# Attention with chunk selection and a top-1 expert layer: longer runs for the loads of Q, K and the second expert weights, a regrouping on GpSimd, and two weight tensors

## The chip, the cores and the metric

The kernel runs on one core of one Trainium2 chip. The metric is the device time of one execution in microseconds. Before the change nine runs were timed; their median is the time before.

A core has five engines that run side by side: TensorE (PE; its weight loads are PEld), VectorE (DVE), ScalarE (ACT), GpSimd (POOL) and SyncE (SP), which here only issues transfers. The transfers of all queues go over 16 transfer engines (DMA).

## The reference

Inputs: q, k, v of 4 batches x 8 heads x 768 tokens x 64; a gate of 512 x 8; for each of 8 experts a first weight matrix of 512 x 1024 and a second one of 1024 x 512, all float32.

```
k_min, k_max = min and max of k over each chunk of 32 tokens
ub    = sum_d max(q * k_min, q * k_max)          # a bound for each query and chunk
top   = the 6 chunks with the largest bound, among chunks not after the query's own
attn  = softmax of q k^T / 8 over the tokens of those chunks up to the query
x     = attn @ v, heads side by side             # 3072 tokens x 512
e     = argmax(x @ w_gate);  g = softmax(x @ w_gate)[e]
out   = g * (relu(x @ w1[e]) @ w2[e])            # one expert per token
```

## The kernel before

Attention goes by pairs of heads: 16 pairs (4 batches x 4), one step of the loop at line 886 for each (pair 0 is written out above it). Within a step for pair i the program interleaves three pairs. For pair i it computes scores (TensorE, L427), their exponentials (ScalarE, L432), the causal mask of the diagonal blocks (GpSimd, L440) and the product with V (TensorE, L455). For pair i+1 it computes the bounds (TensorE, L374), the choice of chunks (VectorE) and the turn of V (L276). For pair i+2 it turns K and Q with TensorE transposes (L227, L245), takes the chunk minima and maxima out of PSUM with VectorE (L235, L236), and evicts K and Q with ScalarE and VectorE (L239, L250, L265). Scores come in seven tiles a pair, units 0 to 6; only tiles 0, 1, 5 and 6 have masks.

K, Q and V of a pair are loaded by SyncE (L201 to L218), one transfer per head. Partition p of tile t holds token 128 t + p, so every run in memory is one row of 64 floats, 256 B. K and Q have two buffers each, by the parity of the pair: pair i+4 is loaded as soon as pair i+2 has been turned, two steps before its use. Even pairs use a tile of their own; odd pairs use space in `w_all` that belongs to the last expert and is filled with weights later.

The expert weights are loaded by GpSimd, which converts them to bf16 on the way (L186 to L195): 32 loads, four per expert, each of 1 MB in HBM; the first two of an expert bring w1 in rows of 1024, the last two w2 in rows of 512. All land in the one tensor `w_all`. A list gives each load a slot; there are four slots a step:

```
many = [4 + n * 44 // 19 for n in range(19)]
wq = [0, 1, 2, 3] + many + [48, 50, 51, 52, 54, 55, 56, 57, 58]
```

When a batch's four pairs are done, its tokens are routed: logits, gate and rank (VectorE, with small matmuls), and then six scatters (GpSimd, L561) write the rows of x to `xs_dram`, sorted by expert. For the first three batches they are spread over the next batch's steps.

GpSimd and TensorE run in the order that the program is written in; so do VectorE and ScalarE in the first part, and VectorE in the loop. GpSimd's order in a step is: three masks (tiles 0 and 1 of pair i), two casts `q_c` (L257), a cast `q_d` (L268), then by slots a weight load and a scatter, the mask of tile 5, again weight load and scatter, the two masks of tile 6, and again.

The expert layer takes tiles of 128 sorted rows: GpSimd gathers them (L666), SyncE turns them with a transfer (L678), `up` multiplies by w1 (L699), ScalarE applies relu (L707), a transfer turns the result (L711), `down` multiplies by w2 two tiles later (L755), ScalarE scales by the gate (L761), and GpSimd scatters the rows to the output (L739). Which expert a tile belongs to is read from a table into a register, which selects the weights at run time. The last tile of the 28 that always run is handled in halves (L703 to L736).

Of the kernel before, what the change touches and what calls it, by code (L numbers as in the profile page):

```python
# [24 lines left out]
def kernel(  # L25
# [34 lines left out]
    VW = D + 1 + E  # L60
    LK = max(NT * 2 * D, 3 * XW // 2)
# [6 lines left out]
    w_all = wpool.tile([128, E * WE], BF16)  # L68
# [117 lines left out]
    def load_w(s_):  # L186
        e, n = divmod(s_, 4)
        if n < 2:
            dst = w_all[:, ds(e * WE + n * 2 * F, 2 * F)].rearrange("p (c f) -> p c f", c=2)
            src = moe_w1[e, ds(n * 256, 256)]  # L190
        else:
            dst = w_all[:, ds(e * WE + W1W + (n - 2) * 4 * DM, 4 * DM)].rearrange("p (c f) -> p c f", c=4)
            src = moe_w2[e, ds((n - 2) * 512, 512)]
        d = nc.gpsimd.dma_start(out=dst, in_=src.rearrange("(c p) f -> p c f", p=128))  # L194
        tc.keep_in_program_order(d)  # L195
# [5 lines left out]
    def load(i, nm):  # L201
        if i >= NP:
            return
        b, hp = divmod(i, HP)
        if nm in "kq" and i % 2:
            at = (E - 1) * WE + (W1W + 4 * DM if nm == "k" else 2 * F)
            t_ = w_all[:, ds(at, NT * 4 * D)].bitcast(FP32).rearrange("p (t a d) -> p t a d", a=2, d=D)
        elif nm == "k":
            t_ = ld.tile([128, LK], FP32, tag=nm, name=nm)
            t_ = t_[:, 0:NT * 2 * D].rearrange("p (t a d) -> p t a d", a=2, d=D)  # L210
        elif nm == "q":
            t_ = ld.tile([128, NT, 2, D], FP32, tag=nm, name=nm)
        else:
            t_ = V[i % 3][:, :, 1 + E:1 + E + 2 * D].rearrange("p t (a d) -> p t a d", d=D)
        for hd in range(2):
            nc.sync.dma_start(out=t_[:, :, 1 - hd if nm == "v" else hd, :],
                              in_=dict(k=k, q=q, v=v)[nm][b, 2 * hp + hd].rearrange("(t p) d -> p t d", p=128))
        st[i][nm] = t_  # L218

    def prep_steps(i):  # L220
# [3 lines left out]
        def k_t(hf):  # L224
            pt = ps_m.tile([128, 384], FP32, tag="m")
            for t in range(3):
                nc.tensor.transpose(pt[:, ts(t, 128)], s["k"][:, 3 * hf + t], ident_f[:])  # L227
            s[f"kp{hf}"] = pt

        def k_red(hf):  # L230
            if hf == 0:
                s["kmx"] = work.tile([128, NCH], FP32, tag="kmx", name="kmx")
                s["kmn"] = work.tile([128, NCH], FP32, tag="kmn", name="kmn")
            v_ = s[f"kp{hf}"][:].rearrange("p (c w) -> p c w", w=CH)
            nc.vector.tensor_reduce(s["kmx"][:, ts(hf, 12)], v_, AX.X, ALU.max)  # L235
            nc.vector.tensor_reduce(s["kmn"][:, ts(hf, 12)], v_, AX.X, ALU.min)  # L236

        def k_out(hf, hd):
            nc.scalar.activation(kte[0:64, hd, ts(hf, 384)], s[f"kp{hf}"][64 * hd:64 * hd + 64, :],  # L239
                                 AF.Copy, bias=0.0, scale=0.125)  # L240

# [6 lines left out]
        def q_v(hf):  # L248
            qT = s[f"qT{hf}"] = work.tile([128, 384], FP32, tag=f"qT{hf}", name="qT")
            nc.vector.tensor_copy(out=qT[:], in_=s[f"qp{hf}"][:])  # L250
# [12 lines left out]
        def q_va(hf):  # L263
            qT = s[f"qT{hf}"] = work.tile([128, 384], FP32, tag=f"qT{hf}", name="qT")
            nc.scalar.activation(qT[:], s[f"qp{hf}"][:], AF.Copy)  # L265
# [35 lines left out]
        def first(idle):  # L301
# [11 lines left out]
            for hf in range(2):  # L313
                s[f"qT{hf}"] = work.tile([128, 384], FP32, tag=f"qT{hf}", name="qT")
                qA = s[f"qA{hf}"] = work.tile([128, 384], FP32, tag=f"qA{hf}", name="qA")
                nc.scalar.activation(qA[:], s[f"qp{hf}"], AF.Relu)
                if hf == 0:
                    nc.scalar.activation(s["qT0"][:], s["qp0"], AF.Copy)
                else:
                    nc.vector.tensor_copy(out=s["qT1"][:], in_=s["qp1"])  # L320
# [139 lines left out]
    def norm(i, hf):  # L460
        b, hp = divmod(i, HP)
        s = st[i]
        if hf == 0:
            s["lgt"] = work.tile([128, 3, 2, 2, E], FP32, tag="lgt", name="lgt", bufs=2)
            if hp == 0:
                bst[b]["lg"] = work.tile([128, 3, 2, E], FP32, tag="lg", name="lg", bufs=2)
                for h in range(2):
                    if b % 2 == 0 or h:
                        t_ = work.tile([128, 3, XW], BF16, tag=f"xrow{b % 2}{h}", name="xrow")[:]
                    elif b < B - 1:  # L470
                        at = (E - 1) * WE + W1W
                        t_ = w_all[:, ds(at, 3 * XW)].rearrange("p (t x) -> p t x", x=XW)
# [109 lines left out]
    def table(first):  # L582
# [25 lines left out]
        nc.vector.tensor_scalar(woff[:, cols], ej[:], float(WE), None, ALU.mult)  # L608
# [43 lines left out]
    def gather(j):  # L652
# [9 lines left out]
        elif j == 2:  # L662
            spare = ld.tile([128, 2, 768], BF16, tag="q", name="spare")
# [27 lines left out]
    def up(j):  # L691
        _, (wo,) = nc.values_load_multi_w_load_instructions(
            woff[0:1, j:j + 1], engines=[PE], min_val=0, max_val=(E - 1) * WE,
# [3 lines left out]
        for c in range(NDC):  # L697
            for fh in range(F // 512):
                nc.tensor.matmul(ph[:, fh, :], lhsT=xT[:, c, :],  # L699
                                 rhs=w_all[:, ds(wo + (c * F + fh * 512), 512)],  # L700
                                 start=(c == 0), stop=(c == NDC - 1), skip_group_check=True)
        h_ = work.tile([128, F], BF16, tag="P", bufs=6)
        if j == JM - 1:  # L703
            nc.scalar.activation(h_[:, 0:512], ph[:, 0], AF.Relu)
            nc.vector.tensor_scalar(h_[:, 512:F], ph[:, 1], 0.0, None, ALU.max)
        else:
            nc.scalar.activation(h_[:].rearrange("p (a f) -> p a f", a=2), ph[:], AF.Relu)  # L707
# [16 lines left out]
    def down_last():  # L724
# [4 lines left out]
        for n in range(2):  # L729
            py = (ps_m.tile([128, w], FP32, tag="m", name="py") if n else  # L730
                  ps_o.tile([128, w], FP32, tag="o", name="py"))
            for c in range(NFC):
                nc.tensor.matmul(py[:], lhsT=hT[:, c, :], rhs=w_all[:, ds(wo + (W1W + c * DM + n * w), w)],
# [12 lines left out]
    def down(j, mid=None):  # L746
# [5 lines left out]
        for c in range(NFC):  # L752
            if mid and c == 5:
                mid()
            nc.tensor.matmul(py[:], lhsT=hT[:, c, :], rhs=w_all[:, ds(wo + (W1W + c * DM), DM)],  # L755
# [12 lines left out]
    many = [4 + n * 44 // 19 for n in range(19)]  # L768
    wq = [0, 1, 2, 3] + many + [48, 50, 51, 52, 54, 55, 56, 57, 58]

    def weights(slot):
        for n in range(NW):
            if wq[n] == slot:
                load_w(n)
# [18 lines left out]
    with tc.manual_schedule(engines=MAN):  # L793
# [5 lines left out]
        with tc.manual_schedule(engines={DVE, ACT}):  # L799
# [3 lines left out]
            load(1, "v")  # L803
            load(2, "k")
            load(2, "q")
# [11 lines left out]
            p["k_t"](1)  # L817
            load(3, "k")
# [9 lines left out]
            p["q_t"](1)  # L828
# [258 lines left out]
```

## Time and profile before

| what | value |
| --- | --- |
| median of 9 runs | 367.48 us (361.55 to 373.47) |
| the profiled execution | 367.15 us, span 365.4 us |
| mean granted clock of TensorE | 0.973 |
| busy in the span | TensorE 325.4, weight loads 243.2, ScalarE 199.5, GpSimd 177.0, VectorE 175.1 us |
| packets | 137148, 59.92 MB |
| attention, to about 250 us | 16 steps, 12.9 to 16.8 us each between 20 and 216 us |
| expert layer, from about 250 us | 28 tiles, 3.45 us each at 318 to 350 us |

How to read the lines: a slice row has 40 digits, each the busy share of 1/40 of the span in tenths. A window line has the stretch, its length, the busy time of each engine with its instructions, the granted clock, the share of the transfer engines' time in which packets were under way (outstanding packets can make it more than 1), and the GB/s. A waits line names the engine and line that waited, what it waited for, the total, the count and the longest. A timeline line has start, duration, engine, line, operation, output and inputs, and in brackets the idle time before it and what ended it. "issue" stands for a wait that the profile shows no cause for.

### The profile page before, as it was taken

What the parts mean: (1) busy time and instruction counts of PE and PEld (TensorE: products, weight loads), DVE (VectorE), ACT (ScalarE), POOL (GpSimd) and SP (SyncE); (2) the same over time, 40 slices, a digit from 0 to 9 for tenths busy, and PEclk for the clock granted to TensorE, in tenths of its full rate; (3) what the DMA queues carried; (4) which work ended last, traced back from release to release, by engine and by line L of the source; (5) the groups of instructions that cost most, each with busy time, mean ns of one, the idle gap of its engine ahead of it and who ended that gap; (6) DMA issues with size and microseconds to landing.
All of it is one profiled execution on the core that took longest, in us unless ns stands there. A gap on an engine that the chain in (4) does not pass through costs nothing.

```text
span 365.4 us, 13315 instructions
## 1 busy us (share of the span) xinstructions
PE 325.4 (89%) x5321; PEld 243.2 (67%) x5333; DVE 175.1 (48%) x725; ACT 199.5 (55%) x339; POOL 177.0 (48%) x316
## 2 busy tenths in 40 slices
PE   7899897999999999999999869558999979999980
PEld 3689787898899889889989758435434434444440
DVE  6779476375875777876686737204700000000010
ACT  3778675565866865866774825212244434445440
POOL 7355326052376354366546386640656554654331
PEclk9999999899999999999999999968999999999996
DMA  9999999686989998999976795971989798989830
GB/s 178 194 207 165 218 197 201 128 153 127 173 160 158 196 186 158 169 163 162 200 142 109 148 125 111 183 165 31 180 178 226 165 179 215 186 225 170 207 98 25
DMA packets 137148, 59.92 MB, mean 164 GB/s; under 512 B 121723, under 2 KB 129917, under 8 KB 137088
## 3 DMA queue, kind: packets, MB, share of 16 engines
q0 software_dynamic: 17536, 29.42, 43.1%
q1 hardware_dynamic: 119552, 29.65, 42.5%
q8 instruction: 44, 0.72, 0.8%
q14 instruction: 16, 0.13, 0.1%
HBM read 56.14 MB, written 10.51 MB: 182 GB/s over the span
## 4 chain that ended last, share of the span: by engine, by line
PE 51%; issue 22%; POOL 11%; DVE 6%; DMA 4%; ACT 3%; POOLq 1%; SPq 0%; DVEq 0%; ACTq 0%
PE po L455 22%; PE ps L427 9%; PE ubp L374 5%; POOL out_dram L739 4%; PE vwp L292 3%; PE pt L276 3%; PE pt L245 3%; PE pt L227 3%; DMA xs_dram<-xrow,sli 2%; POOL xs_dram L561 2%; ACT KTE L239 2%; POOL xg L666 1%; ACT P L432 1%; DMA q<-in_q_dram 1%; POOL spare L666 1%
## 5 line engine op out<-in xcount | busy, mean ns | idle before, releaser
L432 ACT ACTIVATE P<-ps 128x768 f32<-128x768 f32 x144 | 89.6, 666 | 69.0 <-PE ps L427 53.2
L455 PE MATMUL po<-V,P 128*64 128x73 f32 x2688 | 108.8, 230 | 13.6 <-issue 7.5
L455 PEld LDWEIGHTS po<-V,P 128*64 128x64 f32 x2688 | 101.9, 138 | 22.5 <-issue 11.3
L440 POOL TENSOR_SCALAR_AFFINE_SELECT P<-P 128x256 f32<-128x256 f32 x90 | 34.6, 406 | 54.1 <-ACT P L432 40.3
L427 PE MATMUL ps<-QSB,KTE 128*64 128x384 bf16 (+2 forms) x576 | 55.9, 296 | 0.5 <-issue 0.5
L755 PE MATMUL py<-w_all,hT 128*128 x211 | 50.4, 379 | 0.9 <-DMA hT<-h__5481 0.3
L239 ACT ACTIVATE KTE<-pt 64x384 bf16<-64x384 f32 x64 | 30.9, 483 | 16.5 <-DVE kmn L236 9.2
L755 PEld LDWEIGHTS <-hT 128*128 128x128 bf16 x216 | 21.0, 98 | 26.9 <-issue 1.2
L561 POOL DMA_INDIRECT xs_dram<-xrow,sli x21 | 21.5, 1026 | 28.1 <-DVE cnt L586 14.0
L699 PE MATMUL ph<-w_all,KTE 128*128 x116 | 29.6, 394 | 3.3 <-issue 1.8
L427 PEld LDWEIGHTS <-KTE 128*64 128x64 bf16 x576 | 29.1, 111 | 4.8 <-issue 3.6
L402 DVE COPY QSB<-pm 24x768 bf16<-24x768 bf16 x30 | 16.5, 550 | 17.7 <-PE pm L398 17.2
L699 PE MATMUL ph<-w_all,QSB 128*128 x102 | 24.3, 379 | 0.6 <-issue 0.5
L194 POOL DMA_DIRECT2D w_all<-in_moe_w_dram x32 | 24.6, 770 | 0.2
L480 DVE RECIPROCAL rec<-po 128x6 f32<-128x6 f32 x32 | 6.2, 195 | 38.3 <-PE po L455 24.5
L374 PE MATMUL ubp<-KS,qT 128*64 128x48 f32 x384 | 24.1, 224 | 0.5 <-issue 0.4
L699 PEld LDWEIGHTS <-KTE 128*128 128x128 bf16 x120 | 11.9, 100 | 18.4 <-issue 4.8
L374 PE MATMUL ubp<-KD,qA 128*64 128x48 f32 x384 | 23.7, 222 | 0.4 <-issue 0.4
L739 POOL DMA_INDIRECT out_dram<-V,ti x14 | 13.8, 985 | 18.7 <-ACT V L761 17.4
L374 PEld LDWEIGHTS ubp<-KS,qT 128*64 128x64 f32 x384 | 20.0, 137 | 3.3 <-issue 2.5
L374 PEld LDWEIGHTS ubp<-KD,qA 128*64 128x64 f32 x384 | 20.1, 138 | 0.5 <-issue 0.5
L276 PE MATMUL pt<-ident_f,V 128*128 128x128 f32 x96 | 16.2, 283 | 3.1 <-ACT qT L265 2.6
(208 smaller groups left out, 474.2 us busy)
## 6 DMA issues: line engine op xcount, KB each, us to landing
w_all<-in_moe_w_dram POOLq DMA_DIRECT2D x32, 512.0 KB
V<-in_v_dram SPq DMA_DIRECT2D x32, 192.0 KB
k<-in_k_dram SPq DMA_DIRECT2D x16, 192.0 KB
q<-in_q_dram SPq DMA_DIRECT2D x16, 192.0 KB
w_all<-in_k_dram SPq DMA_DIRECT2D x16, 192.0 KB
w_all<-in_q_dram SPq DMA_DIRECT2D x16, 192.0 KB
xs_dram<-xrow,sli POOLq DMA_INDIRECT x21
out_dram<-V,ti POOLq DMA_INDIRECT x14
```

Source lines behind the costliest of these rows:

```text
L194: d = nc.gpsimd.dma_start(out=dst, in_=src.rearrange("(c p) f -> p c f", p=128))
L239: nc.scalar.activation(kte[0:64, hd, ts(hf, 384)], s[f"kp{hf}"][64 * hd:64 * hd + 64, :], AF.Copy, bias=0.0, scale=0.125)
L276: nc.tensor.transpose(pt[:, ts(t, 128)], V[i % 3][:, 3 * hf + t, 1 + E:1 + E + 2 * D], ident_f[:])
L374: nc.tensor.matmul(pu[c:c + CW, 3 * hf + t].rearrange("p a n -> p (a n)"), lhsT=s[f"{nm}{hf}"][:, ds(t * 128 + c, CW)], rhs=w_[:], start=( ...
L427: nc.tensor.matmul(pv[c:c + CW, hd, :], lhsT=kte[:, hd, ds(kb * 128 + c, CW)], rhs=qsb[:, hd, ds(qb * 384 + 384 - w, w)], start=True, stop ...
L432: nc.scalar.activation(P[:, :, ds(c0, w)], pv, AF.Exp)
L440: nc.gpsimd.affine_select(out=pd, in_=pd, pattern=[[0, 2], [1, 128]], compare_op=ALU.is_ge, fill=0.0, base=0, channel_multiplier=-1)
L455: nc.tensor.matmul(po[c:c + CW, t].rearrange("p a d -> p (a d)")[:, ds(hd * VW, VW)], lhsT=P[:, hd, ds(col + c, CW)], rhs=vt[:, kb, ds((1 ...
L561: d = nc.gpsimd.indirect_dma_start(out=xs_dram[:], out_offset=bass.IndirectOffsetOnAxis(ap=sli[:, u:u + 1], axis=0), in_=bst[b][f"xrow{u % ...
L699: nc.tensor.matmul(ph[:, fh, :], lhsT=xT[:, c, :], rhs=w_all[:, ds(wo + (c * F + fh * 512), 512)], start=(c == 0), stop=(c == NDC - 1), sk ...
L739: d = nc.gpsimd.indirect_dma_start(out=out[:], out_offset=bass.IndirectOffsetOnAxis(ap=ti[:], axis=0), in_=y, in_offset=None, bounds_check ...
L755: nc.tensor.matmul(py[:], lhsT=hT[:, c, :], rhs=w_all[:, ds(wo + (W1W + c * DM), DM)], start=(c == 0), stop=(c == NFC - 1))
```

## The change

- K and Q are loaded in longer runs. K of a head comes in two transfers: tokens 0 to 511 with four rows of 64 in a run, so that partition p holds tokens 4p to 4p+3, and tokens 512 to 767 with two. Q comes in two transfers with three rows each. In memory a run is 1024, 512 or 768 B.
- For pairs from 1 on the runs land in a buffer with heads outermost (`outer`), and GpSimd copies them into one with the heads side by side for each row (`inner`, by `spread`); pair 0 is written there directly, in pieces of 256 B. There is now one buffer to land in and one to turn from, for K and for Q. The copy for pair i+3 stands in step i, behind the transposes of pair i+2, and the load of pair i+4 follows it.
- Since tokens are now spread over partitions in runs, the transposed columns are out of order; the evictions of K and Q write them with steps, and the chunk reductions read them with steps. K's two PSUM tiles hold 512 and 256 columns instead of 384 each.
- `w_all` is split into `w1_all` and `w2_all`. w2 is loaded so that a partition gets four neighbouring rows, 8 KB in one run; relu therefore reads its PSUM tile with a step of four, to bring the hidden units into the same order.
- The weight loads go out in another order (first weights, then second; those of the last expert that lie over the K and Q buffers last), and in evenly spaced slots: 1, 2, 4, 6, 8, 10, 11, 13, ... 47, 49, 51, 53, 55, 57.
- In the last tile the two halves of the output swap the PSUM pools that they use.

The diff, cut to its core:

```diff
-    w_all = wpool.tile([128, E * WE], BF16)
+    w1_all = wpool.tile([128, E * W1W], BF16)
+    w2_all = wpool.tile([128, E * W1W], BF16)
...
-            dst = w_all[:, ds(e * WE + W1W + (n - 2) * 4 * DM, 4 * DM)].rearrange("p (c f) -> p c f", c=4)
-            src = moe_w2[e, ds((n - 2) * 512, 512)]
+            dst = w2_all[:, ds(e * W1W + (n - 2) * 4 * DM, 4 * DM)]
+            src = moe_w2[e, ds((n - 2) * 512, 512)].rearrange("(p c) f -> p (c f)", p=128)
...
+            for lo, n in RUNS[nm]:
+                tok_ = src[128 * lo:128 * (lo + n)]
+                if i == 0:
+                    nc.sync.dma_start(out=t_[:, lo:lo + n, hd], in_=tok_.rearrange("(p t) d -> p t d", t=n))
+                else:
+                    nc.sync.dma_start(out=t_[:, hd, lo:lo + n].rearrange("p t d -> p (t d)"),
+                                      in_=tok_.rearrange("(p t) d -> p (t d)", t=n))
+    RUNS = dict(k=((0, 4), (4, 2)), q=((0, 3), (3, 3)))
...
+    def spread(i, nm):
+        if i >= NP:
+            return
+        dense = st[i][nm]
+        st[i][nm] = inner(nm)
+        nc.gpsimd.tensor_copy(out=st[i][nm].rearrange("p t a d -> p a t d"), in_=dense)
...
+            v_ = s[f"kp{hf}"][:].rearrange("p (s c w) -> p c s w", s=n, w=CH // n)
+            nc.vector.tensor_reduce(s["kmx"][:, c], v_, AX.XY, ALU.max)
...
+            nc.scalar.activation(kte[0:64, hd, ds(128 * lo, 128 * n)].rearrange("p (w s) -> p s w", s=n),
+                                 s[f"kp{hf}"][64 * hd:64 * hd + 64, :].rearrange("p (s w) -> p s w", s=n),
...
+            nc.vector.tensor_copy(out=in_order(qT[:]), in_=as_read(s[f"qp{hf}"][:]))
...
-            nc.scalar.activation(h_[:].rearrange("p (a f) -> p a f", a=2), ph[:], AF.Relu)
+            nc.scalar.activation(h_[:].rearrange("p (a c f) -> p a c f", a=2, c=4),
+                                 ph[:].rearrange("p a (f c) -> p a c f", c=4), AF.Relu)
...
-            py = (ps_m.tile([128, w], FP32, tag="m", name="py") if n else
-                  ps_o.tile([128, w], FP32, tag="o", name="py"))
+            py = (ps_o.tile([128, w], FP32, tag="o", name="py") if n else
+                  ps_m.tile([128, w], FP32, tag="m", name="py"))
...
+    first_w = [4 * e + n for e in range(E) for n in (0, 1)]
+    second_w = [4 * e + n for e in range(E) for n in (2, 3)]
+    order_w = first_w[:-1] + second_w[:-2] + first_w[-1:] + second_w[-2:]
...
+            if 1 + n * 56 // (NW - 1) == slot:
+                load_w(order_w[n])
...
             if pj:
                 pj["k_t"](0)
                 pj["k_t"](1)
-                load(i + 4, "k")
...
             scores(i, 2)
+            spread(i + 3, "k")
+            load(i + 4, "k")
...
+            spread(i + 3, "q")
+            load(i + 4, "q")

             scores(i, 4)
```

## The prediction

> **What bounds the kernel now.** I read the page's busy shares and slices first, then the transfer queues, then windows cut at each attention step (from one head pair's bound matmuls, line 374, to the next's), then the waits and timeline of the stretches that stood out.
>
> ```profile
> PE 325.4 (89%) x5321; PEld 243.2 (67%) x5333; DVE 175.1 (48%) x725; ACT 199.5 (55%) x339; POOL 177.0 (48%) x316
> ...
> PE   7899897999999999999999869558999979999980
> ...
> PEclk9999999899999999999999999968999999999996
> DMA  9999999686989998999976795971989798989830
> ```
>
> TensorE is the bound; the transfer engines are close to full beside it, and no other engine is over 55%. So a cheaper transfer pays only where TensorE stands still because of transfers. The windows show where that may be (columns: stretch, length, busy time of PE, PEld, DVE, ACT, POOL, granted clock, transfer share, GB/s):
>
> ```profile
> 31.80:46.70 14.90, 13.29 (x303) 11.93 (x302) 8.99 (x36) 9.25 (x17) 7.11 (x18) 1.00 1.19 213
> ...
> 60.30:77.00 16.70, 14.37 (x303) 13.55 (x302) 8.98 (x36) 9.38 (x17) 5.52 (x14) 0.90 0.71 133
> 105.00:118.10 13.10, 13.03 (x302) 12.13 (x304) 9.05 (x36) 9.64 (x19) 8.78 (x19) 1.00 0.98 179
> ...
> 198.90:215.70 16.80, 12.70 (x294) 11.12 (x294) 10.93 (x47) 8.52 (x16) 9.80 (x15) 1.00 0.81 147
> 229.40:249.40 20.00, 12.62 (x130) 7.82 (x131) 3.15 (x11) 4.11 (x6) 8.94 (x11) 0.75 0.71 150
> ```
>
> A step with the same 303 matmuls takes 13.1 us when nothing disturbs it (105.0) and 14.9 or 16.7 us early on. The waits of TensorE from 44 to 77 us say what for:
>
> ```profile
> PE po L455 <- issue: 2.8, 2, 2.3
> PE vwp L292 <- issue: 1.4, 1, 1.4
> ```
>
> "issue" is a wait for nothing shown. Both long ones (1.42 us before 45.16, 2.33 us before 64.65) fall while the transfer share is over 1 and SyncE needs 9.66 us to issue one pair of V loads (29.64). I read them as TensorE's own instructions coming late through the full transfer engines. It is a reading; no row proves it.
>
> **Part 1, the transfers.** The queue rows:
>
> ```profile
> DMA packets 137148, 59.92 MB, mean 164 GB/s; under 512 B 121723, under 2 KB 129917, under 8 KB 137088
> ...
> q0 software_dynamic: 17536, 29.42, 43.1%
> q1 hardware_dynamic: 119552, 29.65, 42.5%
> ```
>
> From 105 to 118.1 us q1 moved 4704 packets in 42.1% of 13.1 us: 5.5 us of all 16 engines per step, 18.8 ns x engine per 256 B packet (13.6 B/ns). Weights from 20 to 45 us: 3.01 MB, 5.74 loads of 0.52 MB, in 72.6% of 25 us, so 3.16 us each; one reads 1 MB, 20.7 B/ns. K and Q of a step are 786 KB: 3.6 us at the first rate, 2.4 us at the second; packets of 512 to 1024 B lie between, I take 3.0. That is 0.6 us a step off the transfers. W2 in 8 KB runs falls from 512 to 128 packets a load, and gets 0 to 10% cheaper by the same two rates.
>
> Of more weight is when the weights go. Slots (four a step): before 0,1,2,3,4,6,8 ... 54,55,56,57,58; after 1,2,4,6,8 ... 51,53,55,57. Two of the first four loads leave step 0 (6.3 us of transfers off the backlog at 30 to 60 us), and the last full step issues one load, not three. The middle gets denser, some 2.2 loads a step where 1.7 were: 7.0 us, with K and Q 3.0, V 1.8 (1536 packets) and a scatter or two of 0.5 comes to 12.3 us a step of 13.1, or 13.2 with K and Q at 3.6. So a loss there is bounded by 0.1 us x 8 steps, about +1; I take 0.
>
> A, early stalls: three steps from 31.8 to 77 us last 45.2 us; at 13.2 each they would last 39.6. Between 0 and 5.6 us are to be had; I take -4.0, as the transfer share there (1.19, 1.13) should come to about 1.
> B, end of attention: three loads issued at 223.5 to 225.5 fill the engines until 233.8 (q0 89.5% from 229 to 238 us), and TensorE loses 0.46, 0.21 and about 1.1 us to "issue" there and some 1.3 us behind it. 0 to -3; taken -2.0. The next stretch, 238.7 to 244.7 us, has 24 matmuls with gaps near 0.7 us between them, beside gathers and transposes that the change leaves alone: taken 0, but up to -7 with the clock of 0.5 to 0.75 that follows.
> D, step 13: GpSimd issues a weight load at 209.73, then two scatters, and its masking at 213.14 is what TensorE waited 2.80 us for. That load moves one slot up, where GpSimd waits 4.34 us for the gate anyway. -0.8 (one issue, 0.77 us); bounds 0 and -1.1.
>
> **Part 2, the regrouping on GpSimd.** Thirty copies of 128x768 f32. Nearest rows: cast 64x384 0.496 us (L257), mask 128x256 0.406, memset 64x768 0.73. From the first two, 0.7 ns per element over 0.23 us: 0.77 us; with strides I take 0.9, bounds 0.7 and 2.0 (four L257 casts). 30 x 0.9 = 27 us on an engine that is busy 177 of 365. Its cover is the idle time between casts and masks (3.9 us at 119.3). Each copy waits for its loads, the transposes that read the old data, and GpSimd's order; masks, weight issues and scatters queue behind it, and the next K or Q load on SyncE waits for it. A load is now issued one step ahead instead of two, so 12 us cover its landing. Where scatters precede, the cover is thin:
>
> ```profile
> 118.38 0.94 POOL L257 CAST QSB<-qT 64x384 bf16<-64x384 f32 x2
> 123.23 0.50 POOL L268 CAST QSB<-qT 64x384 bf16<-64x384 f32 x1 [3.90 <-DMA xs_dram<-xrow,sli]
> 123.69 0.78 POOL L194 DMA_DIRECT2D w_all<-in_moe_w_dram  x1
> 124.78 1.05 POOL L561 DMA_INDIRECT xs_dram<-xrow,sli  x1 [0.30 <-issue]
> 127.06 1.25 POOL L440 TENSOR_SCALAR_AFFINE_SELECT P<-P 128x256 f32<-128x256 f32 x3 [1.24 <-ACT P L432]
> ```
>
> The cast waits for the scatters to land; after it now come weight issue, copy, scatter, copy: 123.73 + 0.78 + 0.9 + 1.35 + 0.9 = 127.7 where the mask is due at 127.06: 0.6 us late. The steps at 105, 159 and 171.9 have casts ending 2.1, 1.5 and 0.2 us earlier in their steps, so 0, 0 and 0.4. Steps 5 and 9 scatter without that wait, 0 to 0.3. G: +1.0 (bounds 0 and +9: with copies of 2.0 us the six steps lose 2.8, 0.7, 1.3, 2.6, 1.0, 1.0).
>
> **Part 3, the start.** K and Q of pair 0 need eight issues instead of four before TensorE can turn Q. An issue takes 0.52 us (1.04 for two): last one ends at 5.0 instead of 3.0. But 786 KB at the 215 GB/s of that stretch take until 5.7 anyway, and Q was awaited at 6.7: F +0.4, bounds 0 and +2.0. The copies of pair 1 end near 10.7 and 12.4 us by the same rate; its K transposes run at 12.21, its Q transposes at 16.81.
>
> **Part 4, reordered elements.** K evictions (L239, 0.483 us), Q evictions (L250, 0.557; L265, 0.487) and K reductions (0.552) keep their element counts but write or read with steps; relu (L707, 1.023 us) reads PSUM at every fourth element. The trace has no long stepped eviction; the nearest, the reciprocal of 128x6 at step 73, takes 0.195 us against 0.17 for six packed elements. So 0, and at the other end a doubling, which lies beside other work: ScalarE is busy 9.1 to 9.6 of 13.1 us a step, and a tile's transpose is issued at 322.83 for matmuls at 328.49, 5.7 us later with a transfer of 1.23 us to issue.
>
> [...]
>
> E, the tail: the last two output halves swap their PSUM pools.
>
> ```profile
> 353.31 0.69 ACT L761 ACTIVATE V<-py,xg 128x512 f32<-128x512 f32 x1 [0.23 <-PE ph L718]
> ...
> 354.05 2.31 PE L733 MATMUL py<-w_all,hT 128*128 x16 [0.99 <-ACT V L761]
> ```
>
> The first half now takes a free bank and starts at 353.1; the second, 1.15 us later, finds the old one evicted at 354.0: -0.95. A slower last relu (0.60 to 1.2 us) hides before the turn at 351.80. Splitting the weight tensors frees nothing: the last load has landed by 234, the first expert matmul runs at 245.9.
>
> **Sum.** A -4.0, B -2.0, D -0.8, E -0.95, F +0.4, G +1.0: -6.35. The profiled execution took 367.15 us (span 365.4), 0.33 below the median of 367.48, so 360.8 for it and 361 at the median. The nine runs spread from 361.55 to 373.47, so I call 1% what can be told from no change.
>
> A rule that speaks against A and B: the Trainium skill, "Runtime: NRT & Kernel Launch", Instruction fetch mechanics, says that fetches in 16 KiB blocks are hidden behind execution. The two gaps of 1.42 and 2.33 us under full transfers agree better with late fetches; by the rule A and B are nothing and the sum is 366.8.
>
> **Rivals.**
> 1. The stalls stay (A and B at 0): TensorE's gaps were not the transfers', or the denser middle brings as many as leave. For it: gaps at 207.4 and 208.1 us with the transfer share at 0.25. Time 367.15 - 0.35 = 366.8.
> 2. Slower: GpSimd becomes the pace in the six scatter steps. Place: the copy of Q ahead of the mask of the fifth score tile. Each microsecond past 127.06 in the example goes to TensorE, six times. It decides from 1.2 us more per step than planned (7.35 us: the gain of 6.35 and the 1 us already counted), by copies of 2 us or scatters landing later behind denser weights. At 2 us: 360.8 + 12 = 373. Against it: the L257 rate, and the other seven steps with copies have casts that end 1 us after they start and no scatter to wait for.
> 3. Faster still: the stretch 238.7 to 244.7 us also heals: 361 - 7 = 354.
>
> **Chances.** Forecast (356 to 363.8) 0.48; stalls stay (363.8 to 371) 0.24; GpSimd paces (over 371) 0.21; faster still 0.07. Faster by over 1% is below 363.8: 0.55; within 1%: 0.24; slower, above 371.2: 0.21. The range leaves out one in ten at each end: 354 (rival 3) to 374 (rival 2 at its price).
>
> **What will show it.** A: steps from 31.8 to 77 us near 13.3 us, "issue" waits of TensorE shorter. B: no matmul gaps from 228 to 235 us, q0 low there. G: copies of 0.7 to 1.0 us; TensorE's wait for masks (3.0 us before) up by about 1. E: no wait before the last 16 matmuls. Q1 with 32768 packets fewer. Wrong would make it: copies near 2 us, or copies waiting for loads longer than a step, or step times as uneven as before with less transfer share.

## The result and the profile after

The changed kernel takes 394.6 us (median of 10 runs, 391.1 to 400.57), beside 367.2 us for the kernel before (31 runs): a ratio of 1.079, interval 1.0748 to 1.0832. The forecast was 361.0 with a range of 354 to 374. The profiled execution took 389.96 us, span 388.2.

The runs below were made on four chips, and the median of the kernel before was 355 to 369 us by chip. So kernels are compared on one chip, by their ratio to the kernel before. Each ratio is taken from the fast runs of both kernels, and so differs a little from the ratio of the medians.

From the page after: the busy shares, the slices of TensorE, its clock and the transfers, and the queues.

```profile
PE 334.6 (86%) x5321; PEld 248.8 (64%) x5333; DVE 177.9 (46%) x725; ACT 229.8 (59%) x339; POOL 198.5 (51%) x346
...
PE   6887898898979889879898797795789999999994
...
PEclk9898999988989999999899899998699999999999
DMA  5755977958576889687668674547259999999971
...
DMA packets 101310, 59.94 MB, mean 154 GB/s; under 512 B 76667, under 2 KB 92029, under 8 KB 101248
...
q0 software_dynamic: 11392, 29.42, 38.8%
q1 hardware_dynamic: 89856, 29.66, 36.2%
```

The transfers became cheaper: 35838 packets fewer, both queues less busy. In q1 it is 29696 packets fewer, where 32768 were forecast; pair 0, which still lands in pieces of 256 B, is part of the difference. ScalarE gained 30.3 us of work (199.5 before), GpSimd 21.5 (177.0). TensorE's share fell, and the loss is in attention. The windows after, cut at the bounds of one pair and the next (stretch, length, PE, PEld, DVE, ACT, POOL, clock, transfer share, GB/s):

```profile
70.10:86.60 16.50, 14.65 (x302) 12.91 (x301) 9.10 (x36) 11.29 (x17) 7.18 (x16) 0.90 0.77 154
121.00:135.90 14.90, 13.06 (x303) 11.80 (x302) 9.02 (x36) 11.07 (x19) 9.53 (x17) 1.00 0.79 169
...
231.30:247.90 16.60, 12.35 (x297) 11.04 (x296) 11.32 (x47) 10.39 (x16) 9.13 (x14) 1.00 0.51 98
```

An undisturbed step (121.0) now takes 14.9 us for the same 303 matmuls, where it took 13.1, with the transfer engines at 0.79 instead of 0.98 and ScalarE at 11.1 us instead of 9.6. TensorE's waits from 11.7 to 248 us say for what:

```profile
PE pt L316 <- ACT qT L305: 20.3, 13, 1.6
PE pt L285 <- ACT KTE L272: 5.8, 12, 1.0
PE pt L316 <- ACT KTE L272: 2.3, 1, 2.3
PE po L495 <- issue: 1.6, 1, 1.6
```

Before, from 8.7 to 216 us, the waits for ScalarE's evictions of K and Q were 3.0 us together:

```profile
PE pt L276 <- ACT qT L265: 2.6, 4, 0.7
...
PE pt L276 <- ACT KTE L239: 0.4, 1, 0.4
```

Now they are 28.4. The groups of ScalarE, by form, before (L239 evicts K, L265 evicts Q) and after (L272, L305):

```profile
L239 ACT ACTIVATE KTE<-pt 64x384 bf16<-64x384 f32 x64 | 30.9, 483 | 16.5 <-DVE kmn L236 9.2 <-PE ubp L374 6.1 <-PE pt L227 0.7
...
L265 ACT ACTIVATE qT<-pt 128x384 f32<-128x384 f32 x15 | 7.3, 487 | 1.8 <-PE pt L245 1.5
```

```profile
L272 ACT ACTIVATE KTE<-pt 64x512 bf16<-64x512 f32 x32 | 42.4, 1324 | 18.9 <-DVE kmn L268 18.5
...
L272 ACT ACTIVATE KTE<-pt 64x256 bf16<-64x256 f32 x32 | 14.6, 457 | 0.5
...
L305 ACT ACTIVATE qT<-pt 128x384 f32<-128x384 f32 x15 | 10.3, 687 | 1.7 <-PE pt L285 1.7
```

The same 24576 columns of K cost 57.0 us instead of 30.9. The form of 512 writes every fourth bf16, that of 256 every second. The timeline of ScalarE after, from 196 to 206 us, shows where that falls:

```profile
197.25 1.57 ACT L472 ACTIVATE P<-ps 128x768 f32<-128x768 f32 x3 [2.36 <-PE ps L467]
199.93 3.62 ACT L272 ACTIVATE KTE<-pt 64x512 bf16<-64x512 f32 x4 [1.10 <-DVE kmn L268]
203.57 1.51 ACT L472 ACTIVATE P<-ps 128x768 f32<-128x768 f32 x2
204.97 0.68 ACT L305 ACTIVATE qT<-pt 128x384 f32<-128x384 f32 x1
```

TensorE in the same stretch:

```profile
203.60 0.55 PE L316 MATMUL pt<-ident_f,V 128*128 128x128 f32 x3
205.71 0.55 PE L316 MATMUL pt<-ident_f,V 128*128 128x128 f32 x3 [1.56 <-ACT qT L305]
```

K's four evictions are one block of 3.62 us, then two exponentials, then Q's eviction. The second turn of V needs a PSUM buffer of the pool that K, Q and V share (`ps_m`, three buffers), and gets it when Q has left, at 205.65. ScalarE is far from full, but it works through this chain in order, and TensorE waits at its end.

### The profile page after: what moved, and what is told of

Its sections match the earlier page's. It is cut to its first block, busy times and chain, and to the rows that moved or that the text cites. A ratio compares the mean times of both kernels' runs of the same rounds, so it can differ in the third digit from the quotient of the medians.

```text
span 388.2 us, 13462 instructions
## 1 busy us (share of the span) xinstructions
PE 334.6 (86%) x5321; PEld 248.8 (64%) x5333; DVE 177.9 (46%) x725; ACT 229.8 (59%) x339; POOL 198.5 (51%) x346
## 3 DMA queue, kind: packets, MB, share of 16 engines
q0 software_dynamic: 11392, 29.42, 38.8%
## 4 chain that ended last, share of the span: by engine, by line
PE 42%; issue 19%; ACT 15%; POOL 10%; DVE 6%; DMA 4%; another core or an unknown queue 1%; SPq 1%; POOLq 1%; ACTq 0%; DVEq 0%
PE po L495 19%; PE ps L467 8%; ACT KTE L272 6%; ACT P L472 6%; POOL out_dram L782 4%; DMA xs_dram<-xrow,sli 3%; PE ubp L414 3%; PE pt L285 3%; PE pt L316 2%; PE pt L257 2%; PE vwp L332 2%; ACT qT L305 2%; POOL xg L706 2%; DVE kmx L267 2%; DVE kmn L268 1%
## 5 line engine op out<-in xcount | busy, mean ns | idle before, releaser
L495 PE MATMUL po<-V,P 128*64 128x73 f32 x2688 | 111.3, 236 | 8.8 <-DVE rec L519 4.0
L495 PEld LDWEIGHTS po<-V,P 128*64 128x64 f32 x2688 | 106.0, 144 | 17.4 <-issue 10.5
L272 ACT ACTIVATE KTE<-pt 64x512 bf16<-64x512 f32 (+1 forms) x64 | 57.0, 890 | 19.4 <-DVE kmn L268 18.5
L480 POOL TENSOR_SCALAR_AFFINE_SELECT P<-P 128x256 f32<-128x256 f32 x90 | 34.6, 407 | 59.7 <-ACT P L472 59.4
L467 PE MATMUL ps<-QSB,KTE 128*64 128x384 bf16 (+2 forms) x576 | 57.9, 304 | 0.2 <-issue 0.2
L316 PE MATMUL pt<-ident_f,V 128*128 128x128 f32 x96 | 17.9, 304 | 23.5 <-ACT qT L305 20.3
L600 POOL DMA_INDIRECT xs_dram<-xrow,sli x21 | 21.5, 1026 | 25.8 <-DVE cnt L625 13.4
L467 PEld LDWEIGHTS <-KTE 128*64 128x64 bf16 x576 | 30.2, 114 | 4.4 <-issue 3.9
L739 PE MATMUL ph<-w_all,KTE 128*128 x116 | 28.8, 386 | 1.3 <-DMA KTE<-more_x 0.5
L316 PEld LDWEIGHTS pt<-ident_f,V 128*128 128x128 f32 x96 | 10.5, 146 | 30.1 <-ACT qT L305 23.4
L326 DVE COPY vT<-pt 128x384 f32<-128x384 f32 x29 | 15.8, 552 | 19.4 <-PE pt L316 19.4
L739 PEld LDWEIGHTS <-KTE 128*128 128x128 bf16 x120 | 11.8, 100 | 15.8 <-issue 2.9
L196 POOL DMA_DIRECT2D w_all<-in_moe_w_dram x32 | 21.0, 657 | 0.0
```

Source lines behind the costliest of these rows:

```text
L196: d = nc.gpsimd.dma_start(out=dst, in_=src)
L272: nc.scalar.activation(kte[0:64, hd, ds(128 * lo, 128 * n)].rearrange("p (w s) -> p s w", s=n), s[f"kp{hf}"][64 * hd:64 * hd + 64, :].rear ...
L316: nc.tensor.transpose(pt[:, ts(t, 128)], V[i % 3][:, 3 * hf + t, 1 + E:1 + E + 2 * D], ident_f[:])
L467: nc.tensor.matmul(pv[c:c + CW, hd, :], lhsT=kte[:, hd, ds(kb * 128 + c, CW)], rhs=qsb[:, hd, ds(qb * 384 + 384 - w, w)], start=True, stop ...
L480: nc.gpsimd.affine_select(out=pd, in_=pd, pattern=[[0, 2], [1, 128]], compare_op=ALU.is_ge, fill=0.0, base=0, channel_multiplier=-1)
L495: nc.tensor.matmul(po[c:c + CW, t].rearrange("p a d -> p (a d)")[:, ds(hd * VW, VW)], lhsT=P[:, hd, ds(col + c, CW)], rhs=vt[:, kb, ds((1 ...
```

## Experiments

Theory S: the steps with which K and Q are written cost ScalarE time, and the chain above passes it on. Rival G: the copies on GpSimd, or the longer path of the loads, make the steps longer, and the waits for ScalarE follow from that.

**K packed.** The changed kernel, with K evicted in the order in which it is read. K's columns are then in the wrong order.

```diff
-  kte[0:64, hd, ds(128 * lo, 128 * n)].rearrange("p (w s) -> p s w", s=n),
-  s[f"kp{hf}"][64 * hd:64 * hd + 64, :].rearrange("p (s w) -> p s w", s=n),
+  kte[0:64, hd, ds(128 * lo, 128 * n)],
+  s[f"kp{hf}"][64 * hd:64 * hd + 64, :],
```

> The changed kernel with K's evictions written packed, in the order of the PSUM tile, so K's columns are in the wrong order and the scores are of the wrong tokens; all else as changed. Theory S (the stepped bf16 writes of K on ScalarE, 1.324 us for 512 columns, hold up the exponentials and the Q eviction, for which TensorE waits 1.6 us in each of 13 steps): K evictions fall to about 0.60 and 0.38 us, steps from 14.9 to about 13.5 us, time to about 375 us. Rival G (the GpSimd copies and the loads one step ahead set the pace): steps stay at 14.9, time 391 to 397 us.

Measured 365.71 us, ratio 1.0009 (0.9936 to 1.0081). This is what S says, and more of the loss went than expected (375 us). The copies were all still there, so G does not explain the loss. Q was still written with steps (0.693 us at L305, f32 at a step of 12 bytes).

**Read step.** The same permutation, but the step is on the side that is read: K and Q are read from PSUM 512 B apart and written side by side.

```diff
-  kte[...].rearrange("p (w s) -> p s w", s=n), s[...].rearrange("p (s w) -> p s w", s=n)
+  kte[...].rearrange("p (w s) -> p w s", s=n), s[...].rearrange("p (s w) -> p w s", s=n)
```

> The changed kernel with the reordering moved to the read side: evictions of K and Q read PSUM with steps of 512 B and write SBUF packed; it computes the reference. Theory S, if stepped PSUM reads are as cheap as the relu's (1.023 us before and after): evictions at the packed durations (0.60, 0.38, 0.49, 0.56 us), steps near 13.2 us, time 366 to 370 us. Theory S, if reads with a step cost as much as writes: 390 to 397 us with evictions still near 1.3 us. Rival G: 391 to 397 us with evictions at the packed durations.

Measured 366.07 us, ratio 1.0003 (0.9946 to 1.0059). This version computes the reference. Its groups for K:

```profile
L272 ACT ACTIVATE KTE<-pt 64x512 bf16<-64x512 f32 x32 | 18.9, 592 | 19.1 <-DVE kmn L268 18.8
...
L272 ACT ACTIVATE KTE<-pt 64x256 bf16<-64x256 f32 x32 | 12.1, 378 | 0.5
```

Here reading with a step costs nothing (0.592 us, and 0.593 us with packed reads in the run before this one), while writing with one cost 1.324. Against the profile after, ScalarE has 29.7 us less to do (229.8 to 200.1), and the way from the first pair's bounds to the last one's takes 213.3 us instead of 236.2. So 22.9 of 29.7 us had reached TensorE. Its waits for these evictions fell from 28.4 to 4.8 us. Not all of the difference is waiting: TensorE's busy time fell too, from 334.6 to 326.2 us, at a mean granted clock of 0.970 instead of 0.956. That Q's steps went too made no difference that these runs can tell.

**Before, K stepped.** The kernel before with one edit: K's four evictions of 384 write every fourth bf16, which also puts K's columns in a wrong order.

```diff
-  kte[0:64, hd, ts(hf, 384)], s[f"kp{hf}"][64 * hd:64 * hd + 64, :],
+  kte[0:64, hd, ts(hf, 384)].rearrange("p (w s) -> p s w", s=4),
+  s[f"kp{hf}"][64 * hd:64 * hd + 64, :].rearrange("p (s w) -> p s w", s=4),
```

> The kernel before with one part of the change alone: K's evictions written with a step of four bf16 (8 B), which puts K's columns in a wrong order. Theory S: an eviction of 384 columns goes from 0.483 to about 1.05 us (2.2 ns per column over 0.2 us), steps gain 1 to 2 us, time 380 to 390 us. Rival G: evictions longer but hidden beside other work, time within 1% of the kernel before, 364 to 371 us.

Measured 401.5 us, ratio 1.0961 (1.08 to 1.1122). The eviction alone makes the old kernel slower than the whole change did. Group and wait:

```profile
L239 ACT ACTIVATE KTE<-pt 64x384 bf16<-64x384 f32 x64 | 65.7, 1026 | 15.6 <-DVE kmn L236 9.1 <-PE ubp L375 6.1
```

```profile
PE pt L277 <- ACT KTE L239: 19.6, 14, 1.9
```

ScalarE has 34.8 us more to do here, and the whole takes 34.6 us more (401.5 against 366.93). That the two agree so well is chance: TensorE's waits for ScalarE grew by some 27 us (3.2 to 30.2 us up to 250 us), and its busy time by 16.3 us (325.4 to 341.7) at a granted clock of 0.935 instead of 0.973, while other waits became shorter. GpSimd has no copies here, so G is not needed for the loss.

**Probe of steps.** No attention: evictions of 64x512 f32 from PSUM, four of each kind, ScalarE (L41) and VectorE (L44); the output is zeros. The number of x in a name is the step in elements, b is bf16 and f is f32, `write` or `read` the side with the step.

> A kernel that computes nothing of the reference and writes zeros: evictions of 64x512 f32 from PSUM by ScalarE and by VectorE, packed, written with steps of 2, 4 and 8 elements (bf16 and f32), and read with steps. Theory S: ScalarE bf16 write packed about 0.60 us, step 2 about 0.7, step 4 about 1.3, step 8 longer; stepped reads near 0.60. Rival G needs nothing of it. If all forms take 0.60 us, the 1.324 us in the changed kernel is contention and not the step.

```profile
L41 ACT ACTIVATE abwritexxxxxxxx<-pa 64x512 bf16<-64x512 f32 x4 | 9.8, 2447 | 0.1
L44 DVE CAST dbwritexxxxxxxx<-pd 64x512 bf16<-64x512 f32 x4 | 9.7, 2421 | 0.1
L41 ACT ACTIVATE abwritexxxx<-pa 64x512 bf16<-64x512 f32 x4 | 5.2, 1296 | 0.1
...
L41 ACT ACTIVATE afwritexxxx<-pa 64x512 f32<-64x512 f32 x4 | 4.3, 1068 | 0.1
...
L41 ACT ACTIVATE abwritexx<-pa 64x512 bf16<-64x512 f32 x4 | 2.9, 732 | 0.1
...
L41 ACT ACTIVATE afwritexx<-pa 64x512 f32<-64x512 f32 x4 | 2.5, 615 | 0.1
...
L41 ACT ACTIVATE abwritex<-pa 64x512 bf16<-64x512 f32 x4 | 2.4, 590 | 0.2
...
L41 ACT ACTIVATE abreadxxxx<-pa 64x512 bf16<-64x512 f32 x4 | 2.3, 587 | 0.1
```

With bf16, steps of 4, 8 and 16 bytes cost 1.24, 2.2 and 4.1 times the packed write; with f32, steps of 8 and 16 bytes 1.05 and 1.8 times. VectorE comes to nearly the same times for bf16 at 8 and 16 bytes (1.280 us at 8 bytes, 0.682 packed). Reads with a step take 0.587 to 0.672 us on ScalarE (0.590 packed) and 0.677 to 0.732 us on VectorE. So the probe has, without any other work beside it, the 1.324 against 0.592 us of the kernel.

That settles the slowdown, but not the forecast: without the stepped writes the change is worth nothing, where 6 us were forecast. The next runs take it apart. "Packed" is the read-step version from here. The theories T, U and V stand in the expectation of the next run.

**Weights part alone**, on the kernel before: both tensors, 8 KB runs with the reordered ReLU, order and slots, swapped banks.

> The kernel before with the weights part alone: two tensors, second weights in 8 KB runs with the reordered ReLU output, the new order and the even slots (the load into Q's old region one slot late, at 54, so that the region is free), the swapped banks of the tail; queries and keys loaded and evicted as before. Theory T (the weights part carries what the packed versions gained at the end): from the start of the last step to the end 140 us as in the packed versions, against 149.6 before, and the steps before it unchanged, so 355 to 360 us. Rival U (the end was shorter for another reason, such as the copies having moved work out of it): 364 to 370 us and 147 to 150 us from the start of the last step. Rival V (the loads now spread over all steps slow the scatters and the loads of keys and queries): the end gains, but steps 3 to 14 give back 5 us or more.

Measured 345.38 us, ratio 0.9722 (0.9648 to 0.9796), on a chip on which the kernel before took 356.22. By the ratio that is 357 us on the first chip, inside the range of T. From the last pair's bounds to the end it takes 127.7 us. There is no profile of the kernel before from this chip, so where the gain lies is left to the last comparison below.

**Schedule alone**: the same without 8 KB runs and reordered ReLU.

```diff
-  dst = w2_all[:, ds(...)];  src = moe_w2[...].rearrange("(p c) f -> p (c f)", p=128)
+  dst = w2_all[:, ds(...)].rearrange("p (c f) -> p c f", c=4);  src = moe_w2[...].rearrange("(c p) f -> p c f", p=128)
```

> The same as the run of the weights part alone, but the second weights are still read in 2 KB runs and the ReLU writes its output in order: only the two tensors, the order, the slots and the swapped banks are left. If the spread of the loads over the steps is what shortens the end: within 2 us of the weights part alone. If the run length does it (a quarter of the packets for the second weights): the end goes back to 146 to 150 us and the time to 363 to 369 us.

Measured 352.14 us, ratio 0.9837 (0.9738 to 0.9935): between the two expectations. In the profiles 4.1 us of the difference lie behind the last scatter (8.36 us to the end, 4.25 with the 8 KB runs).

**Keys and queries alone, packed**: the other half of the change.

> The packed version (PSUM read with a step, packed writes) with the weight loads, their layout, order and slots and the tail's banks as in the kernel before: the part on queries and keys alone, without the stepped writes. Computes the reference. If the two parts add up: time before plus what the packed version lost ahead of the last step, +7 us, and the end as before: 372 to 377 us. If the part on queries and keys is worth nothing either way: 364 to 370 us. If it is what shortens the end: 355 to 362 us.

Measured 357.88 us, ratio 1.0153 (1.0038 to 1.0269): by itself, this part loses, even without stepped writes; by the ratio some 5 us where 7 were expected.

**Copy ahead of the cast.** In the packed version TensorE waits in step 12 (see below). One move in GpSimd's order:

```diff
+  spread(i + 3, "k"); load(i + 4, "k")
   pn["q_d"](1)
   ...
-  spread(i + 3, "k"); load(i + 4, "k")
```

> The packed version with one move in GpSimd's order: the copy of K (and the load behind it) is issued ahead of the cast of the query half, which waits in the scatter steps for the scatters to land, instead of behind it. Computes the reference. If the last batch's row tile, which lies in K's landing buffer, is what made step 12 last 19.1 us (the copy of the last pair stood behind the waiting cast, and the norm behind the copy): step 12 goes to 13.5 to 15 us and the time to 359 to 362 us. If step 12 is long for the waiting scatters themselves: step 12 stays at 18 to 20 us and the time at 364 to 368 us.

Measured 347.02 us, ratio 0.977 (0.9673 to 0.9866), without the packed version beside it. So both were run on one chip, with the kernel before as a third.

> The kernel before, unchanged, as one of the compared kernels: a ratio of 1.00 shows how far the comparison itself can be trusted (expected within 0.7% of 1), and its profile gives the steps on the same chip as the three others. In the first profile of it the last step's start to the end took 149.6 us, with matmuls of the last step 0.7 us apart from 238.7 to 244.7 us. If that stretch belongs to the kernel (the burst of weights at the end of attention): 145 us or more again. If it belongs to something that comes and goes: 125 to 140 us.

> The packed version (both parts of the change, PSUM read with a step, packed writes) on one chip with the version that copies K ahead of the cast. If that order is worth what its step 12 showed: this one 1 to 3% slower than that one, with a ratio to the kernel before of 0.99 to 1.005. If the gap between the two came from the chips they ran on: both at the same ratio, within 1%.

> The packed version with the copy of K ahead of the cast, on one chip with the packed version itself. Order worth 1 to 3%: ratio to the kernel before 0.97 to 0.985. Order worth nothing: the packed version's ratio, within 1%.

The kernel before against itself: 1.0006 (0.9957 to 1.0055). Packed: 0.9992 (0.9952 to 1.0031). Copy ahead: 0.985 (0.9784 to 0.9917). By these ratios the order is worth 1.4% (1.1% by the medians, 364.58 and 360.68 us). GpSimd's timeline in step 12, packed:

```profile
186.35 0.94 POOL L297 CAST QSB<-qT 64x384 bf16<-64x384 f32 x2
192.85 0.50 POOL L308 CAST QSB<-qT 64x384 bf16<-64x384 f32 x1 [5.55 <-DMA xs_dram<-xrow,sli]
193.42 0.82 POOL L247 COPY w_all<-k 128x768 f32<-128x768 f32 x1
```

VectorE at the same time:

```profile
194.27 0.56 DVE L520 TENSOR_TENSOR xrow<-po,rec 128x384 bf16<-128x384 f32 x1 [4.54 <-POOL w_all L247]
```

The rows `xrow` of the last batch lie in the tile in which K lands (`ld`, tag "k"). The last K is copied out of it by the copy at 193.42, which stands behind a cast that waits 5.55 us for scatters to land. VectorE's normalization waits for the copy, and TensorE 3.2 us for VectorE: the stretch that lies in step 12 takes 18.7 us, 13.5 in the kernel before on the same chip. With the copy moved it stands ahead of that wait, and the stretch takes 15.3 us:

```profile
188.06 0.82 POOL L247 COPY w_all<-k 128x768 f32<-128x768 f32 x1
193.31 0.51 POOL L308 CAST QSB<-qT 64x384 bf16<-64x384 f32 x1 [4.43 <-DMA xs_dram<-xrow,sli]
```

**Early slots.** The kernel before, with the first 23 loads at every second slot.

```diff
-  wq = [0, 1, 2, 3] + many + [48, 50, 51, 52, 54, 55, 56, 57, 58]
+  wq = [1 + n * 46 // 23 for n in range(23)] + [48, 50, 51, 52, 54, 55, 56, 57, 58]
```

> The kernel before with one edit: the first 23 weight loads at every second slot from 1 to 45, instead of four in the first step and then 19 from slot 4 to 45; the nine at the end as before. If the waits of the first five steps come from four weight loads in the first step in front of the loads of keys and values: the first five steps 3 to 5 us shorter (68.3 us before, 63.6 with the weights part alone), time 0.985 to 0.993 of before. If they come from the many short packets of the keys and queries: the steps stay at 67 to 69 us and the ratio at 0.995 to 1.005.

Measured ratio 0.9989 (0.9934 to 1.0045), first five stretches 66.1 us (66.5 in the kernel before on this chip). Two weight loads fewer in the first step gain nothing that these runs can tell.

**What the 8 KB runs do.**

> The weights part alone, 8 KB runs kept, with the ReLU output in its old order (hidden channels then meet the wrong rows of the second weights). Question: TensorE's sequencer reaches the closing barrier 4.4 us late in every profile so far with 2 KB runs and the plain ReLU, and 0.5 us late in every one with 8 KB runs and the reordered ReLU. If the run length of the weights sets it: 0.5 us. If the form of the ReLU sets it: 4.4 us, and some 4 us (1.1%) more than the weights part alone.

> The complement: schedule, split and banks of the weights part with 2 KB runs, but the reordered ReLU output (the same mismatch of hidden channels the other way round). Run length sets the late closing: 4.4 us; ReLU form sets it: 0.5 us. Apart from the closing, steps and feed-forward part within 2 us of the run above; if the 8 KB runs also feed the attention steps better, the last step starts 2 us or more later here.

> The weights part alone, once more, beside the two kernels above. Its ratio to the kernel before was 0.972 on a chip that ran everything 3% faster; if that holds anywhere: 0.965 to 0.985 here, and the closing barrier 0.5 us late. If it was that chip: 0.99 or more. Stretch of matmuls fed 0.7 us apart at the end of attention, seen in five profiles on other chips and in none of the four on that one: if it comes and goes with the chip, it is here or missing in all three runs of this call.

Ratios 0.9763 (0.9632 to 0.9894), 0.9852 (0.9799 to 0.9906) and 0.9724 (0.9651 to 0.9797). In the profiles of the first two the last pair's bounds begin at 214.7 and 214.0 us and the last scatter at 338.34 and 338.65: in this pair the 8 KB runs speed up nothing up to there. (In the earlier pair, the weights part alone and the schedule alone, the last scatter starts at 335.75 and 342.74 us, but the four profiles with 8 KB runs themselves range from 335.75 to 340.42.) Then, at the barrier that closes the program, SyncE waits for TensorE's sequencer (PEq in the rows), with 8 KB runs:

```profile
SPq L1083 <- PEq L1083: 0.9, 2, 0.5
```

and with 2 KB runs:

```profile
SPq L1086 <- PEq L1086: 5.0, 2, 4.4
```

The end comes 4.3 and 8.4 us after the start of the last scatter. All profiles with 17536 packets in q0 show 8.2 to 8.4 us, all with 11392 packets 4.2 to 5.0, whatever else they hold; the form of the ReLU makes no difference. The ratios agree: 0.984 and 0.985 with 2 KB runs, 0.972 to 0.976 with 8 KB, some 4 us. Why TensorE's sequencer is late stays open.

**Before and weights part, side by side.**

> The kernel before, unchanged, for a profile on the same chip as the weights part alone beside it. Ratio 1.00 within 0.7%. Closing barrier 4.4 us late. If the stretch at the end of attention goes with the chip: it is in both profiles or in neither. If it goes with the burst of weights: here and not beside it.

> The weights part alone beside the kernel before. Account expected for the 2.8%, some 10 us: 4.1 us at the closing barrier, 0.8 us for the swapped banks, 3 to 5 us in the first five steps, the rest (0 to 2 us) at the end of attention. If the ratio is 0.99 or more here, its gain needs the chips that ran everything 3% faster.

The weights part alone: 344.15 us, ratio 0.9735 (0.9629 to 0.9841). The spans of the two profiles are 354.0 and 341.6 us. By stretches:

| stretch | before | weights alone | difference |
| --- | --- | --- | --- |
| first five, from 8.8 us | 66.9 | 64.4 | -2.5 |
| the next, to the last pair's bounds | 137.4 | 140.9 | +3.5 |
| to the first expert matmul | 24.7 | 19.5 | -5.3 |
| expert layer, to its last TensorE turn | 102.7 | 99.4 | -3.3 |
| to the start of the last scatter | 5.15 | 4.34 | -0.8 |
| to the end | 8.3 | 4.3 | -4.0 |

TensorE at the end of attention, before:

```profile
232.69 0.53 PE L427 MATMUL ps<-QSB,KTE 128*64 128x256 bf16 x8
237.84 0.59 PE L699 MATMUL ph<-w_all,KTE 128*128 x1 [4.62 <-DMA KTE<-KTE]
238.65 2.76 PE L699 MATMUL ph<-w_all,KTE 128*128 x6 [0.22 <-issue]
```

and with the weights part:

```profile
232.80 0.53 PE L428 MATMUL ps<-QSB,KTE 128*64 128x256 bf16 x8
233.57 1.89 PE L699 MATMUL ph<-w_all,KTE 128*128 x7 [0.24 <-issue]
```

Before, three weight loads issued from 220.9 to 222.9 us lie in front of the gathers (issued at 224.6 and 226.0); the turn of the first gathered rows starts at 233.10, with the weights spread at 227.06:

```profile
233.10 2.66 SPq L678 DMA_TRANSPOSE KTE<-KTE  x2
```

```profile
227.06 2.87 SPq L678 DMA_TRANSPOSE KTE<-KTE  x2
```

TensorE waits 4.62 us for it. That the three loads are what delays the gathers is read from this order; no run moves them alone. The matmuls behind the wait are slower: of the ten of L699 that start from 237.8 to 245.8 us the median takes 631 ns instead of 379, at a granted clock of 0.75 from 237.8 to 250 us. That is most of the 3.3 us in the next row.

The +3.5 us in the middle: the stretch of step 8 (128.2 to 143.6) takes 15.5 us instead of 13.5, steps 12 and 13 take 1.0 and 1.2 us more, and step 11 takes 1.4 us less. TensorE's only wait in step 8 is

```profile
PE po L456 <- issue: 1.7, 1, 1.7
```

In the two other profiles of the weights part alone the same wait is 1.5 and 2.0 us. No row names what TensorE waits for there, but the queue of instructions (q8) tells when its packets of 16 KB move. Before, 36 of them move between 12 and 226 us, one in 5.9 us. In the 18 profiles of whole kernels TensorE has 43 "issue" waits of 0.9 us or more in this time, and each of the 43 ends 2.2 to 3.1 us after such a packet: 2.66 and 2.55 us for the two that the prediction read, 2.44 us for this one. So they look like waits for instructions, as the prediction read them; the rows show the time and not the cause. The rule on instruction fetch that it weighed (the Trainium skill, "Runtime: NRT & Kernel Launch", Instruction fetch mechanics) holds for most blocks here (two such waits for 36 packets, before) and not for all. What makes a block late is open; no run varies it.

## Why the prediction was wrong

- **The step that failed is in Part 4:** "So 0, and at the other end a doubling, which lies beside other work: ScalarE is busy 9.1 to 9.6 of 13.1 us a step". The price was wrong: the stepped write took 1.324 us against 0.592, 2.2 times, on half of K's evictions, and 1.2 times on the rest. The cover was wrong: 22.9 of the 29.7 us reached TensorE. A share of busy time was taken for cover, while the evictions stand in ScalarE's order ahead of exponentials and of Q's eviction, whose PSUM buffer TensorE waits for; the waits for ScalarE's evictions, 3.0 us before, were in the trace. The nearest row (a reciprocal with 6 elements) was too small to show a price per element. The relu, which reads PSUM with a step and writes side by side, did stay at 1.02 us. And the doubling that was named as the other end was never carried into the range.
- **A rule on steps:** the Trainium skill, "SBUF — State Buffer", Door 1, has steps through SBUF free up to 4 fp32 or 8 bf16, and asks for two accesses to each line of 16 bytes. The writes of the probe differ, and the measurement decides: 4 bf16 apart (8 bytes, two in a line) cost 2.2 times, 4 f32 apart (16 bytes, one in a line) 1.8 times; only f32 8 bytes apart was nearly free (1.05 times).
- **Part 1:** by its own terms the dense middle with K and Q at 3.6 us comes to 12.9 us, not 13.2.
- **A (-4.0):** -2.4 and -2.5 us in the two comparisons on one chip (64.0 against 66.5 packed, 64.4 against 66.9 weights alone). The reading of the two long waits as late instructions is supported by the packets of q8. The reason given for a gain, two loads fewer in the first step, does not: the early slots alone gave -0.4. What does it is open. What rival 1 said of the denser middle came true in part: one "issue" wait of 1.5 to 2.0 us is new in step 8.
- **B (-2.0):** too small: -5.3 us and most of the next -3.3 with the clock, in the comparison without the stretch of rival 3. The burst of loads as its cause fits the timeline, but no run isolates it. It was priced by the gaps of the "issue" waits; the wait for the turned rows did not show in that trace. And its "about 1.1 us" is misplaced: the wait of 1.13 us lies at 241.56, in the stretch taken at 0.
- **D (-0.8):** seen where the load was moved. With the load one slot up, the wait of 2.8 us for the mask is 2.07 us in the first run of the packed version and gone in the second, whose step 13 takes 1.92 us less, though an "issue" wait of 2.0 us is new in it. The runs of the weights part alone keep this load in its old slot, 54, and TensorE still waits 2.7 us there.
- **E (-0.95):** -0.8, about as forecast.
- **F (+0.4):** +2.7 us (first bounds at 11.8 us packed, 9.1 before, one chip), beyond its upper bound of 2.0. In the other runs the packed versions had them at 9.8 to 11.9.
- **G (+1.0):** the copies cost 0.82 and 0.84 us (0.9 taken). But what queues behind the waiting cast was followed to the masks only, not to who else uses the landing tile: +5.2 us in step 12.
- **Rival 2** had the sign right by luck: ScalarE, not GpSimd, set the pace. **Rival 3** (the stretch near 240 us heals): on the chips on which the kernel before took 367 us or more, the gaps near 240 us are in all profiles but one, in the packed version as well (244 to 248 us); the one, the first run of the packed version, has a single wait of 7.3 us for VectorE in their place. On the chips on which it took 355 or 356 us they are missing in every profile, with either schedule of the weights. So they go with the chip rather than with the change; why stays open.
- **Not on the list:** 4.0 us at the closing barrier.

Packed against before, on one chip: +2.65 (start) -2.43 (A) +1.46 (middle) +5.18 (step 12) -1.92 (step 13) -1.68 (to the last scatter) -4.06 (close) = -0.80 us of span, 363.0 to 362.2. Gains of 10.1 us (7.75 forecast) stand against losses of 9.3 (1.4 forecast). The parts measured alone, 0.973 and 1.015, would leave -1.2%, where the two together gave 0.0% on other chips; that difference is not settled.

The weights part alone beats both kernels, with 0.972, 0.972 and 0.974 of the time before.

## What to carry to other kernels

On ScalarE and VectorE, put a permutation on the side that is read from PSUM and write side by side; price a new step from a probe of the same shape, on both sides, before the transfers that it pays for. Idle share of an engine is no cover for an operation on which a chain in its order hangs: follow who waits for what is queued behind it, and who else uses the buffer that it frees. Look at what transfers lie ahead of the first one that a new stage needs.

## What the runs showed that was not expected

- Writing 512 columns of bf16 to SBUF every 8 bytes takes 1.3 us, every 16 bytes 2.4 us, on ScalarE and VectorE alike, against 0.59 and 0.68 packed; f32 every 16 bytes takes 1.07 us on either.
- The program's end comes 4 us later when the second weights are loaded in 2 KB runs (17536 packets in q0 instead of 11392), long after the last of these transfers.
- After a wait of 4.62 us, matmuls of TensorE took up to 631 ns instead of 379, at a granted clock of 0.75 over 12 us.
- All 43 longer "issue" waits of TensorE in attention end 2.2 to 3.1 us after a packet of 16 KB in the queue of instructions.
